# First W1 load split, one warm-up product fewer, third V in another bank, last key sums in two parts and scaled on VectorE

## The chip, the core and the metric

The kernel runs on one core of a Trainium2 chip. The core has five engines with instruction queues of their own: TensorE (PE, matrix products, with a weight loader PEld that overlaps it), VectorE (DVE), ScalarE (ACT), GpSimd (POOL) and SyncE (SP, which here only issues transfers). They meet through semaphores alone. The metric is the device time of one execution in microseconds; a kernel's time is the median of its runs.

## What is computed

The input `x` has 2048 tokens of 512 features. Two branches read it, and a gate per token mixes them.

```python
def reference(A_x, A_wqkv, A_w_phi, A_wo, B_x, B_w1, B_w2, gate_w):   # H = 32 heads of 16
    g = sigmoid((A_x * gate_w).sum(-1, keepdims=True))
    q, k, v = split_heads(A_x @ A_wqkv)
    pq, pk = q @ w_phi, k @ w_phi                                     # per head, 16 x 16
    phi_q = concat([softmax(pq), softmax(-pq)])                       # 32 features per head
    phi_k = concat([softmax(pk), softmax(-pk)])
    kv  = einsum("bhsf,bhsd->bhfd", phi_k, v);  z = phi_k.sum(s)
    o   = (phi_q @ kv) / (phi_q @ z + 1e-6)
    a   = merge_heads(o) @ A_wo
    b   = relu(A_x @ B_w1) @ B_w2                                     # 512 -> 1376 -> 512
    return g * a + (1 - g) * b
```

All tensors are bfloat16; sums are kept in fp32.

## The kernel before

Every engine has a list of operations written in program order (`_Plan`). An operation names the events that it waits for (`after`) and the event that it sets (`ev`); `emit` turns them into semaphore waits. So the order on each engine is the order of the calls in the source, and nothing is rescheduled. A waiting operation holds everything behind it on its engine.

PSUM has 8 banks of 512 fp32 columns. `free[bank]` holds the event after which a bank may be written again, as a rule the copy that emptied it. `nextbank()` hands out banks 3, 4 and 5 in turn. Bank 2 is for the value products `vtile`, banks 0 and 1 are for the q and k products of `atile`, and banks 6 and 7 collect kv over the whole loop.

The stages, in the order of PE's queue:

1. Start. `warm(5)`, `gatecol(3)` and `warm(2)` put products of a constant on PE (L209) while the first loads run; nothing reads them. Then `xtr(0)` and `xtr(1)` transpose the first 512 tokens by products with an identity matrix (L217), eight products for each half of them, and DVE and ACT copy the results into `XT` (L225, L229).
2. First part of the dense branch. `slab(t)`, for t from 0 to 3, multiplies rows t of W1 by the first 512 tokens for eight units u of 128 columns (L490). Each unit accumulates in a bank of its own over the four slabs. Every product of slab t waits for the load `w1{t}`, one transfer of 128 rows and 1376 columns (344 KB). The relus follow, then two more units (`hunit`).
3. Value products and weight preparation. `vtile(0)`, four times `pre` (W_qk times the block-diagonal W_phi, L287), `rest(0)`, four times `pre`, `vtile(1, "dve")`, `vtile(2, "dve")` (products L373, copies on DVE L381).
4. The loop over 16 tiles of 128 tokens. `atile(m)` makes the q and k logits (L307), ACT takes exp of plus and minus the logits (L326), and DVE sums the exponentials of the keys over each softmax group (L339, event `zk`), takes the reciprocal (L342, `rz`), and POOL multiplies (L346, `pk`), which gives the key features. DVE then sums the query exponentials (L351) and takes their reciprocal (L356); POOL scales the positive half against the negative (L358, L360). A DMA transpose on SP's queue brings the query features to `PHQ` (L365). Three tiles later `kv(m)` (L395) accumulates phi_k times v, with a column of ones for z. Units of the dense branch are placed between, by the table `mid`.
5. End of the loop. `kv(13)`, `kv(14)` and `kv(15)` lie between the last units of the dense branch (`late`); `gate()` puts three short DVE operations (L417 to L420) and `kvfin()` four (L404, L408) behind the last tile's sums. In tiles 5, 8, 11, 13, 14 and 15 (`split`) the exponentials are four operations, keys first: `epk`, `emk` (plus and minus keys), then `ep`, `em` (queries). In tile 15 alone the multiplication L346 is in two halves, softmax groups 0 to 31 on POOL and 32 to 63 on DVE.
6. Output. For each tile `nd` (query features times kv and z, L427), the division on DVE (L433, L437), a DMA transpose (L443), `finA` (times W_o, L461), `finB` (times W2, L452), the mix on DVE (L475), and the store.

SP's queue issues, in this order: two loads of x, four of W1 (L154), W_phi, WV, two transposing loads of W_qk, three of x, and then the transposes and stores of the stages above. The load of `gate_w` is on ACT's queue.

The lines around the change:

Of the kernel before, what the change touches and what calls it, by code (L numbers as in the profile page):

```python
# [6 lines left out]
ALU = mybir.AluOpType  # L7
AX = mybir.AxisListType
# [49 lines left out]
def bass_gated_mix__linear_kernel_hedgehog__dense_activation_relu__prompt_kernel(  # L58
# [17 lines left out]
    P = 128  # L76
# [17 lines left out]
    with ExitStack() as es:  # L94
# [55 lines left out]
            p.dma("sp", lambda e: e.dma_start(out=XS[:, 2 * h:2 * h + 2, :], in_=xq[:, 2 * h:2 * h + 2, :]),  # L150
                  f"x0{h}", ev=f"x0{h}")

        def loadw1(t):
            p.dma("sp", lambda e: e.dma_start(  # L154
                out=W1[:, t, 0:DFF], in_=B_w1[t * P:(t + 1) * P, :]), f"w1{t}", ev=f"w1{t}")

        p.dma("act", lambda e: e.dma_start(out=GR[:, :], in_=gate_w.rearrange("(j p) -> j p", p=P)), "gr", ev="gr")
        for h in range(2):
            loadx0(h)
        for t in range(NDT):  # L160
            loadw1(t)
        p.dma("sp", lambda e: e.dma_start(
            out=WPS[:, :, :], in_=A_w_phi.rearrange("(g hl) r c -> (hl r) g c", g=NDT)), "wps", ev="wps")
# [43 lines left out]
        def warm(n, cols=512):  # L207
            for _ in range(n):
                p.op("pe", lambda e: e.matmul(PS[:, 4, 0:cols], ones[:, 0:P], ones[:, 0:cols], start=True, stop=True))  # L209
# [20 lines left out]
                         after=[f"xt{nm}{q}"], ev=f"x{nm}2")  # L230
                    free[bank] = [f"x{nm}2"]

        w1all = [f"w1{t}" for t in range(NDT)]

        def relu(c, kt, bank, eng):
            dst, src = HT[:, kt, c * 512:(c + 1) * 512], PS[:, bank, :]
# [9 lines left out]
        def nextbank():  # L246
            rot[0] += 1
            return 3 + (rot[0] - 1) % 3
# [51 lines left out]
        def atile(m):  # L300
            b = m % NB
            first = xready(m // 4) + ([f"pc{i}" for i in range(8)] if m == 0 else [])
            order = [(dt, w) for dt in range(NDT) for w in range(2)]
            if m - 1 in split:
                order = [(dt, w) for w in (1, 0) for dt in range(NDT)]
            for i, (dt, which) in enumerate(order):
                p.op("pe", lambda e, dt=dt, which=which: e.matmul(  # L307
                    PS[:, which, 0:DE], XT[:, dt, m * P:(m + 1) * P], WQK[:, which, dt * DE:(dt + 1) * DE],
                    start=(dt == 0), stop=(dt == NDT - 1)),
                    after=(first if i == 0 else []) + (free[which] if dt == 0 else []),  # L310
                    ev=(f"qk{m}" if i == 7 else None))
            src = PS[:, 0:2, 0:DE].rearrange("p a (h f) -> p a h f", h=H)
            base = b * 8 * D
            busy = [f"tq{m - NB}", f"pk{m - NB}", f"pq{m - NB}"] if m >= NB else []

            def expo(s, w, ev):
                step = (4 * D, 2 * D)[s]
                off = base + s * (2 * D + 16)
                scale = (1.0, -1.0)[s]
                if w is None:  # L320
                    dst = bass.AP(tensor=EB, offset=off, ap=[[EBS, P], [step, 2], [32, H], [1, FE]])
                    s_ = src
                else:
                    dst = bass.AP(tensor=EB, offset=off + w * step, ap=[[EBS, P], [32, H], [1, FE]])
                    s_ = src[:, w, :, :]
                p.op("act", lambda e: e.activation(dst, s_, ACT.Exp, scale=scale),  # L326
                     after=[f"qk{m}"] + busy, ev=ev)

            if m in split:
                for w, nm in ((1, "k"), (0, "")):  # L330
                    expo(0, w, f"ep{nm}{m}")
                    expo(1, w, f"em{nm}{m}")
            else:
                expo(0, None, f"ep{m}")
                expo(1, None, f"em{m}")
            emk = f"emk{m}" if m in split else f"em{m}"
            free[1] = [emk]
            free[0] = [f"em{m}"]
            p.op("dve", lambda e: e.tensor_reduce(  # L339
                ZB[:, b, 64:128], EB[:, b, 2, :].rearrange("p (g f) -> p g f", f=DH), AX.X, ALU.add),  # L340
                after=[emk, f"cst{b}"], ev=f"zk{m}")
            p.op("dve", lambda e: e.reciprocal(SC[:, b, 64:128], ZB[:, b, 64:128]),  # L342
                 after=[f"zk{m}"] + ([f"pk{m - NB}"] if m >= NB else []), ev=f"rz{m}")
            halves = (("pool", 0, 2 * H),) if m < NT - 1 else (("pool", 0, H), ("dve", H, 2 * H))
            for eng, f0, f1 in halves:
                p.op(eng, lambda e, f0=f0, f1=f1: e.tensor_tensor(  # L346
                    EB[:, b, 3, :].rearrange("p (g f) -> p g f", f=DH)[:, f0:f1, :],
                    EB[:, b, 2, :].rearrange("p (g f) -> p g f", f=DH)[:, f0:f1, :],
                    SC[:, b, 64 + f0:64 + f1].unsqueeze(2).to_broadcast([P, f1 - f0, DH]), ALU.mult),
                    after=[f"rz{m}"] + ([f"kv{m - NB}"] if m >= NB else []), ev=f"pk{m}" + ("b" if f0 else ""))  # L350
            p.op("dve", lambda e: e.tensor_reduce(  # L351
                ZB[:, b, 0:64].rearrange("p (h s) -> p h s", s=2),
                bass.AP(tensor=EB, offset=base, ap=[[EBS, P], [32, H], [2 * D + 16, 2], [1, DH]]), AX.X, ALU.add),
                after=[f"em{m}"] + ([f"sc{m - NB}"] if m >= NB else []), ev=f"zq{m}")
            zq = ZB[:, b, 0:64].rearrange("p (h s) -> p h s", s=2)
            p.op("dve", lambda e: e.reciprocal(SC[:, b, 32:64], zq[:, :, 1]),  # L356
                 after=[f"zq{m}"] + ([f"sc{m - NB}"] if m >= NB else []), ev=f"rq{m}")
            p.op("pool", lambda e: e.tensor_tensor(SC[:, b, 0:32], zq[:, :, 0], SC[:, b, 32:64], ALU.mult),  # L358
                 after=[f"rq{m}"], ev=f"sc{m}")
            p.op("pool", lambda e: e.tensor_tensor(  # L360
                EB[:, b, 0, :].rearrange("p (h s f) -> p h s f", h=H, s=2)[:, :, 1, :],
                EB[:, b, 1, :].rearrange("p (h s f) -> p h s f", h=H, s=2)[:, :, 1, :],
                SC[:, b, 0:32].unsqueeze(2).to_broadcast([P, H, DH]), ALU.mult),
                after=[f"sc{m}"] + ([f"tq{m - NB}"] if m >= NB else []), ev=f"pq{m}")
            p.dma("sp", lambda e: e.dma_start_transpose(  # L365
                out=PHQ[:, :, m * P:(m + 1) * P], in_=EB[:, b, 0, :]),
                f"tq{b}", after=[f"pq{m}", f"cst{b}"] + (["pm7"] if m == 12 else []), ev=f"tq{m}")

        def vtile(m, eng="act"):
            b = m % VB  # L370
            bank = 2
            for dt in range(NDT):
                p.op("pe", lambda e, dt=dt: e.matmul(  # L373
                    PS[:, bank, :], XT[:, dt, m * P:(m + 1) * P], WV[:, dt, :],
                    start=(dt == 0), stop=(dt == NDT - 1)),
                    after=((xready(m // 4) + ["wv"] + free[bank]) if dt == 0 else ()),
                    ev=(f"v{m}" if dt == NDT - 1 else None))
            dst, src = VS[:, b, :, 0:64], PS[:, bank, :].rearrange("p (g c) -> p g c", g=NG)
            after = [f"v{m}"] + ([f"kv{m - VB}"] if m >= VB else [])
            if eng == "dve":  # L380
                p.op("dve", lambda e: e.tensor_copy(dst, src), after=after, ev=f"cv{m}")  # L381
            else:
                p.op("act", lambda e: e.activation(dst, src, ACT.Copy), after=after, ev=f"cv{m}")  # L383
            free[bank] = [f"cv{m}"]

        def kv(m):
            b = m % NB
            vb = m % VB
            for g in range(NG):
                after = []  # L390
                if g == 0:
                    after = [f"pk{m}", f"cv{m}", f"one{vb}"] + ([f"pk{m}b"] if m == NT - 1 else [])
                    if m == 0:
                        after += free[6] + free[7]
                p.op("pe", lambda e, g=g: e.matmul(  # L395
                    PS[:, 6 + g // 4, (g % 4) * GW:(g % 4) * GW + 65],
                    EB[:, b, 3, g * P:(g + 1) * P], VS[:, vb, g, 0:65],
                    start=(m == 0 and g % 4 == 0), stop=(m == NT - 1), skip_group_check=True),
                    after=after, ev=(f"kv{m}" if g == NG - 1 else None))
# [88 lines left out]
        def slab(t):  # L488
            for u in range(8):
                p.op("pe", lambda e, u=u: e.matmul(  # L490
                    PS[:, UB[u], :], W1[:, t, u * P:(u + 1) * P], XT[:, t, 0:512],
                    start=(t == 0), stop=(t == NDT - 1)),
                    after=[f"w1{t}", XA[t], XB[t]] + free[UB[u]],
                    ev=(f"h0_{u}" if t == NDT - 1 else None))

        warm(5)
        gatecol(3)
        warm(2)
        xtr(0)
        xtr(1)  # L500
        for b in range(VB):
# [17 lines left out]
        for i in range(4, 8):  # L519
            pre(i)  # L520
        vtile(1, "dve")
        vtile(2, "dve")
        mid = [[(1, 0), (1, 1)], [(1, 2), (1, 3)], [(1, 4), (1, 5)], [(1, 6), (1, 7)], [(1, 8), (1, 9)], [(2, 0)],
               [(1, -1), (2, 1)], [(2, 2), (2, 3)], [(2, 4)], [(2, -1), (2, 5)], [(2, 6), (2, 7)], [(2, 8)],
               [(3, -1), (2, 9)], [(3, 0), (3, 1)], [(3, 2), (3, 3)], []]
# [113 lines left out]
```

## Time and profile before

| | us |
|---|---|
| median of 13 runs | 151.45 |
| lowest and highest | 150.79, 153.94 |
| profiled execution, its own time | 151.68 |
| its span, first to last instruction | 149.9 |
| PE busy in the span | 144.4 |
| DVE, ACT, POOL busy | 92.6, 72.1, 53.6 |

The profile is of one execution. A group of instructions is named by its line, its engine, and what it reads and writes. A matmul's shown length goes on for the time that its result takes through the array, so consecutive ones overlap; the step from start to start is the time that one takes from PE. A wait is put down to the work that ended last before the waiting instruction could go on. The chain that ended last runs back from the final instruction through whatever released each step. "Idle" of an engine that does not set the end costs nothing.

### The profile page before, as it was taken

How to read it: one execution, taken by the hardware profiler on the slowest of the kernel's cores; microseconds unless marked ns; L12 is line 12 of the kernel's file. 1: busy time of each engine (PE TensorE's matmuls, PEld its weight loads, DVE VectorE, ACT ScalarE, POOL GpSimd, SP SyncE). 2: the span in 40 equal slices, each digit the busy share in tenths (PEclk: the TensorE clock that was granted, in tenths of full speed). 3: DMA queues.
4: the chain of work that ended last, by engine and by line, in shares of the span. 5: the costliest groups of instructions: out<-in, count | busy, mean ns of one | idle time of the engine just before them, and what ended most of it. 6: DMA issues, size and time to landing. Idle time of an engine off the chain costs nothing.

```text
span 149.9 us, 2544 instructions
## 1 busy us (share of the span) xinstructions
PE 144.4 (96%) x979; PEld 73.4 (49%) x979; DVE 92.6 (62%) x156; ACT 72.1 (48%) x123; POOL 53.6 (36%) x63
## 2 busy tenths in 40 slices
PE   7799979999999999999999989999999999999992
PEld 2544734444455554645645544545544444444442
DVE  2526852778878678678698895475444555555242
ACT  3306527777778797877878863011222111111150
POOL 2030000777768678877879872000000000000000
PEclk9999999999999999999999999999999999999999
DMA  4999994033328977334743436533333322322312
GB/s 140 326 255 225 208 155 90 0 70 70 74 62 238 232 201 107 70 70 105 42 105 70 105 70 39 105 70 105 74 87 85 74 70 70 74 70 72 83 62 70
DMA packets 44516, 16.11 MB, mean 108 GB/s; under 512 B 39288, under 2 KB 43736, under 8 KB 44504
## 3 DMA queue, kind: packets, MB, share of 16 engines
q1 hardware_dynamic: 44352, 15.92, 49.4%
q8 instruction: 8, 0.13, 0.4%
q10 hardware_dynamic: 152, 0.03, 0.1%
q14 instruction: 4, 0.03, 0.1%
HBM read 4.41 MB, written 2.10 MB: 43 GB/s over the span
## 4 chain that ended last, share of the span: by engine, by line
PE 90%; DMA 3%; DVE 2%; POOL 1%; ACT 1%; SPq 1%; issue 0%
PE PS L452 25%; PE PS L307 17%; PE PS L253 16%; PE PS L373 9%; PE PS L461 9%; PE PS L490 5%; DMA W<-in_B_w_dram 3%; PE PS L427 3%; PE PS L395 2%; PE PS L265 2%; PE PS L287 1%; POOL EB L346 1%; DVE ZB L339 1%; ACT EB L326 1%; DVE WQK L475 1%; SPq L150 1%
## 5 line engine op out<-in xcount | busy, mean ns | idle before, releaser
L452 PE MATMUL PS<-W,HT 128*128 128x512 bf16 (+4 forms) x187 | 40.6, 366 | 0.0
L346 POOL TENSOR_TENSOR EB<-EB,SC 128x1024 bf16<-128x1024 bf16 (+1 forms) x16 | 30.5, 1905 | 26.8 <-DVE SC L342 26.8
L326 ACT ACTIVATE EB<-PS 128x480 bf16<-128x480 f32 (+1 forms) x44 | 30.1, 757 | 16.9 <-PE PS L307 16.9
L466 ACT ACTIVATE TFA<-PS,GT 128x512 bf16<-128x512 f32 x16 | 11.0, 687 | 42.7 <-PE PS L461 36.6
L253 PE MATMUL PS<-XT,W 128*128 128x512 bf16 x128 | 30.7, 379 | 0.0
L307 PE MATMUL PS<-WQK,XT 128*128 128x480 bf16 x128 | 28.5, 366 | 0.0
L339 DVE TENSOR_REDUCE ZB<-EB 128x64 f32<-128x1024 bf16 x16 | 19.5, 1220 | 14.2 <-ACT EB L326 14.2
L475 DVE SCALAR_TENSOR_TENSOR WQK<-PS,OMG,TFA 128x512 bf16<-128x512 f32 (+2 forms) x17 | 12.2, 719 | 23.6 <-ACT TFA L466 22.4
L452 PEld LDWEIGHTS PS<-W,HT 128*128 128x128 bf16 (+1 forms) x187 | 17.0, 98 | 17.4
L239 ACT ACTIVATE HT<-PS 128x512 bf16<-128x512 f32 x35 | 20.3, 617 | 8.3 <-PE PS L490 5.8
L307 PEld LDWEIGHTS PS<-WQK,XT 128*128 128x128 bf16 x128 | 12.5, 98 | 13.8
L351 DVE TENSOR_REDUCE ZB<-EB 128x64 f32<-128x1024 bf16 x16 | 18.6, 1164 | 0.0
L253 PEld LDWEIGHTS PS<-XT,W 128*128 128x128 bf16 x128 | 12.0, 98 | 13.2
L360 POOL TENSOR_TENSOR EB<-EB,SC 128x512 bf16<-128x512 bf16 x16 | 16.9, 1055 | 1.3
L373 PE MATMUL PS<-WV,XT 128*128 128x512 bf16 x64 | 16.4, 379 | 0.8 <-DVE VS L381 0.8
L461 PE MATMUL PS<-WO,OT 128*128 128x512 bf16 x64 | 16.1, 378 | 0.0
L437 DVE TENSOR_TENSOR WQK<-PS,RDEN 128x512 bf16<-128x512 f32 x16 | 11.1, 691 | 0.5
L461 PEld LDWEIGHTS PS<-WO,OT 128*128 128x128 bf16 x64 | 6.1, 97 | 7.2
L342 DVE RECIPROCAL SC<-ZB 128x64 f32<-128x64 f32 x16 | 8.8, 553 | 0.5
L433 DVE RECIPROCAL RDEN<-PS 128x32 f32<-128x32 f32 x16 | 5.6, 350 | 4.7 <-PE PS L427 4.7
L373 PEld LDWEIGHTS PS<-WV,XT 128*128 128x128 bf16 x64 | 5.4, 97 | 5.9 <-DVE VS L381 1.3
L383 ACT ACTIVATE VS<-PS 128x512 bf16<-128x512 f32 x13 | 8.0, 612 | 0.0
(54 smaller groups left out, 88.1 us busy)
## 6 DMA issues: line engine op xcount, KB each, us to landing
out_dram<-WQK SPq DMA_DIRECT2D x15, 128.0 KB, 1.7
W<-in_B_w_dram SPq DMA_DIRECT2D x4, 344.0 KB, 5.7
W<-in_B_w_dram SPq DMA_DIRECT2D x1, 768.0 KB, 4.9
OT<-in_A_x_dram SPq DMA_DIRECT2D x2, 256.0 KB, 3.0
WV<-in_A_wqkv_dram SPq DMA_DIRECT2D x1, 512.0 KB, 7.1
W<-in_B_w_dram SPq DMA_DIRECT2D x1, 512.0 KB, 5.6
WO<-in_A_wo_dram SPq DMA_DIRECT2D x1, 512.0 KB, 3.9
PHQ<-EB SPq DMA_TRANSPOSE x16, 2.8
```

The source lines that it names most:

```text
L239: p.op("act", lambda e: e.activation(dst, src, ACT.Relu), after=[f"h{c}_{kt}"], ev=ev)
L253: p.op("pe", lambda e, t=t: e.matmul(PS[:, bank, :], W1[:, t, kt * P:(kt + 1) * P], XT[:, t, c * 512:(c + 1) * 512], start=(t == 0), stop= ...
L307: p.op("pe", lambda e, dt=dt, which=which: e.matmul(PS[:, which, 0:DE], XT[:, dt, m * P:(m + 1) * P], WQK[:, which, dt * DE:(dt + 1) * DE] ...
L326: p.op("act", lambda e: e.activation(dst, s_, ACT.Exp, scale=scale), after=[f"qk{m}"] + busy, ev=ev)
L339: p.op("dve", lambda e: e.tensor_reduce(ZB[:, b, 64:128], EB[:, b, 2, :].rearrange("p (g f) -> p g f", f=DH), AX.X, ALU.add), after=[emk, ...
L346: p.op(eng, lambda e, f0=f0, f1=f1: e.tensor_tensor(EB[:, b, 3, :].rearrange("p (g f) -> p g f", f=DH)[:, f0:f1, :], EB[:, b, 2, :].rearra ...
L351: p.op("dve", lambda e: e.tensor_reduce(ZB[:, b, 0:64].rearrange("p (h s) -> p h s", s=2), bass.AP(tensor=EB, offset=base, ap=[[EBS, P], [ ...
L360: p.op("pool", lambda e: e.tensor_tensor(EB[:, b, 0, :].rearrange("p (h s f) -> p h s f", h=H, s=2)[:, :, 1, :], EB[:, b, 1, :].rearrange( ...
L373: p.op("pe", lambda e, dt=dt: e.matmul(PS[:, bank, :], XT[:, dt, m * P:(m + 1) * P], WV[:, dt, :], start=(dt == 0), stop=(dt == NDT - 1)), ...
L452: p.op("pe", lambda e, kt=kt, M=M: e.matmul(PS[:, bank, 0:n], HT[0:M, kt, m * P:(m + 1) * P], W2[0:M, kt, cs], start=(kt == 0), stop=(kt = ...
L461: p.op("pe", lambda e, t=t: e.matmul(PS[:, bank, :], OT[:, t, m * P:(m + 1) * P], WO[:, t, :], start=(t == 0), stop=(t == NDT - 1)), after ...
L475: p.op("dve", lambda e: e.scalar_tensor_tensor(out=OSB[:, ob, cs], in0=PS[:, bank, 0:n], scalar=OMG[:, m:m + 1], in1=TFA[:, m % 2, cs], op ...
```

## The change

There are five edits.

- The first W1 slab is loaded in two transfers: columns 0 to 511 (units 0 to 3, event `w10a`, 128 KB) and then columns 512 to 1375 (event `w10`, 216 KB). Products of slab 0 with u below 4 wait for the first alone.
- `warm(2)` becomes `warm(1)`.
- `vtile(2, "dve")` writes the bank that `nextbank()` gives, which is 3 at that place, instead of bank 2. Each later call of `nextbank()` thereby gives the next bank of the three.
- In tile 15 the sum over key groups becomes two operations of half the size: over the plus exponentials after `epk15`, and over the minus exponentials after `emk15`.
- In tile 15 the multiplication of the keys is one operation on DVE over all 64 groups, instead of one half on POOL and one half on DVE; `kv(15)` no longer waits for a second event.

```diff
-        def loadw1(t):
+        def loadw1(t, c0=0, c1=DFF, tag=""):
             p.dma("sp", lambda e: e.dma_start(
-                out=W1[:, t, 0:DFF], in_=B_w1[t * P:(t + 1) * P, :]), f"w1{t}", ev=f"w1{t}")
+                out=W1[:, t, c0:c1], in_=B_w1[t * P:(t + 1) * P, c0:c1]), f"w1{t}{tag}", ev=f"w1{t}{tag}")
...
-        for t in range(NDT):
+        loadw1(0, 0, 4 * P, "a")
+        loadw1(0, 4 * P)
+        for t in range(1, NDT):
             loadw1(t)
...
-        w1all = [f"w1{t}" for t in range(NDT)]
+        w1all = ["w10a"] + [f"w1{t}" for t in range(NDT)]
...
-            p.op("dve", lambda e: e.tensor_reduce(
-                ZB[:, b, 64:128], EB[:, b, 2, :].rearrange("p (g f) -> p g f", f=DH), AX.X, ALU.add),
-                after=[emk, f"cst{b}"], ev=f"zk{m}")
+            zk = ZB[:, b, 64:128].rearrange("p (h s) -> p h s", s=2)
+            ek = EB[:, b, 2, :].rearrange("p (h s f) -> p h s f", h=H, s=2)
+            if m == NT - 1:
+                for s, nm in ((0, "epk"), (1, "emk")):
+                    p.op("dve", lambda e, s=s: e.tensor_reduce(zk[:, :, s], ek[:, :, s, :], AX.X, ALU.add),
+                         after=[f"{nm}{m}", f"cst{b}"], ev=f"zk{m}" if s else None)
+            else:
+                p.op("dve", lambda e: e.tensor_reduce(zk, ek, AX.X, ALU.add),
+                     after=[emk, f"cst{b}"], ev=f"zk{m}")
...
-            halves = (("pool", 0, 2 * H),) if m < NT - 1 else (("pool", 0, H), ("dve", H, 2 * H))
-            for eng, f0, f1 in halves:
-                p.op(eng, lambda e, f0=f0, f1=f1: e.tensor_tensor(
-                    EB[:, b, 3, :].rearrange("p (g f) -> p g f", f=DH)[:, f0:f1, :],
-                    EB[:, b, 2, :].rearrange("p (g f) -> p g f", f=DH)[:, f0:f1, :],
-                    SC[:, b, 64 + f0:64 + f1].unsqueeze(2).to_broadcast([P, f1 - f0, DH]), ALU.mult),
-                    after=[f"rz{m}"] + ([f"kv{m - NB}"] if m >= NB else []), ev=f"pk{m}" + ("b" if f0 else ""))
+            p.op("pool" if m < NT - 1 else "dve", lambda e: e.tensor_tensor(
+                EB[:, b, 3, :].rearrange("p (g f) -> p g f", f=DH),
+                EB[:, b, 2, :].rearrange("p (g f) -> p g f", f=DH),
+                SC[:, b, 64:128].unsqueeze(2).to_broadcast([P, 2 * H, DH]), ALU.mult),
+                after=[f"rz{m}"] + ([f"kv{m - NB}"] if m >= NB else []), ev=f"pk{m}")
...
-        def vtile(m, eng="act"):
+        def vtile(m, eng="act", bank=2):
             b = m % VB
-            bank = 2
...
-                    after = [f"pk{m}", f"cv{m}", f"one{vb}"] + ([f"pk{m}b"] if m == NT - 1 else [])
+                    after = [f"pk{m}", f"cv{m}", f"one{vb}"]
...
-                    after=[f"w1{t}", XA[t], XB[t]] + free[UB[u]],
+                    after=["w10a" if t == 0 and u < 4 else f"w1{t}", XA[t], XB[t]] + free[UB[u]],
...
-        warm(2)
+        warm(1)
...
-        vtile(2, "dve")
+        vtile(2, "dve", nextbank())
```

## The prediction

> **What bounds the kernel now.** I read the page first: TensorE (PE) is busy 144.4 of 149.9 us, and no other engine passes 62%.
>
> ```profile
> PE 144.4 (96%) x979; PEld 73.4 (49%) x979; DVE 92.6 (62%) x156; ACT 72.1 (48%) x123; POOL 53.6 (36%) x63
> ```
>
> So an edit pays only where PE stands still, and costs only where it makes PE stand still. The list of waits, kept to PE and its weight loader, says where that is.
>
> ```profile
> PEld PS L490 <- DMA W<-in_B_w_dram: 1.1, 1, 1.1
> PEld PS L395 <- POOL EB L346: 0.9, 1, 0.9
> PE PS L490 <- DMA W<-in_B_w_dram: 0.9, 1, 0.9
> PE PS L373 <- DVE VS L381: 0.8, 1, 0.8
> PE PS L395 <- POOL EB L346: 0.4, 1, 0.4
> ```
>
> Three places: the first W1 product waits for its load, the third V product for a copy, the last kv product for the scaled keys. The chain that ended last, in order of time (start, length, what), passes through all three.
>
> ```profile
> 1.66 5.01 DMA W<-in_B_w_dram
> 6.72 7.08 PE PS L490 x32
> ...
> 18.90 0.88 PE PS L373 x4
> 19.80 0.70 DVE VS L381
> 20.55 1.04 PE PS L373 x4
> ...
> 84.54 1.04 ACT EB L326 x2
> 85.60 1.23 DVE ZB L339
> 86.86 0.56 DVE SC L342
> 87.49 1.57 POOL EB L346
> 89.11 0.42 PE PS L395 x8
> 89.53 1.73 PE PS L253 x8
> 91.26 0.25 PE PS L427 x8
> ```
>
> From 21.4 to 88.5 us the windows view gives PE 67.1 us busy of 67.1: in the loop the other engines follow PE, so time saved ahead of it reaches the end whole. Matmul lengths include a pipeline tail; the step between starts is what counts: 8 products of 512 columns in 1.73 us are 0.216 us each. The timeline shows the slow start: seven warm-up products start 0.427 us apart, and 16 transposes of 128 columns from 3.94 to 5.54 us, 0.107 us apart, both half speed; the 32 W1 products from 6.72 us step at 0.216. The clock row prints 1.0 throughout because the clock record begins only at 6.52 us.
>
> **Third V in another bank.** vtile(2) wrote bank 2 and waited for vtile(1)'s copy. vtile(1)'s products begin at 18.73 us in the timeline, so PE is free at 18.73 + 4 x 0.216 = 19.59, and vtile(2) starts at 20.55: 0.96 us idle. Its new bank is 3, last emptied by a relu (ACT, 14.70 + 0.60 = 15.30 us), long before. The next customer, atile(0), would start at 19.59 + 0.86 = 20.45 and needs the copies of pre (DVE 17.04 + 2.42 = 19.46, ACT 18.45 + 1.06 = 19.51): ready. vtile(2)'s copy is queued on DVE behind vtile(1)'s and ends near 21.2, ahead of its first user. All later turns of banks 3, 4, 5 move by one and keep their period; finB(0) on bank 4 then waits for a relu two units earlier than before. Gain 0.96, with no cover to lose.
>
> **One warm-up fewer.** It gives 0.43 us of PE time, but the second half of x lands only at 1.19 + 3.5 = 4.69 us (slower of the two loads at L150). The first eight transposes move from 3.94 to 3.54, the second eight only from 4.79 to 4.72. The cast that slab 0 needs (third at L225, ending 5.89) ends near 5.82. By itself this is worth nothing: PE waits for W1 until 6.67. It matters for what follows.
>
> **Slab 0 in two loads.** SP issues one more DMA, 0.43 us (four at L154 in 1.85), so W_phi, WV, the wqk transposes, the x transposes and the later transposes on that queue all go 0.43 later. Cover: the second wqk transpose lands near 9.2 + 6.6 = 15.8, then 16.2, and pre(4), at 17.83, comes at 17.3: 1.1 us of slack. WV (11.1) and Wbd (11.6) have over 3 us. The first x transpose lands at 13.43 + 5.8 = 19.2, then 19.7, and is wanted at 24.07 less 1.5. None shows.
>
> When does the 128 KB part land? The whole 344 KB landed 6.67 - 4.69 = 1.98 us after x, but the four W1 loads then follow 0.98 us apart (1.66 + 5.0 to 3.1 + 6.5, three steps). So 1.0 us of the 1.98 was start cost. The part needs 0.98 x 128/344 = 0.37 us of transfer: 5.06 us if the start cost falls on the second part, 6.06 if on the first, 6.67 if time goes by rows rather than bytes (both parts have 128). I take 5.9, by the nearest row (the whole load, start cost mostly first). Here the Trainium skill speaks against the change: "DMA: Bandwidth & Descriptors", section "Bandwidth", advises batching and gives 0.95 us for 64 KB and 6.15 for 1 MB (issued from GpSimd), about 0.6 us of it fixed. By that rule part one lands near 6.0 and the rest 0.6 late, at 7.3; by the row above, where a load queued behind another shows no such gap, near 6.8. I take the row.
>
> Slab 0 then starts at 5.9 instead of 6.72. The four products that part one feeds run at half speed until the clock opens at 6.52: 0.62 / 0.427 = 1.45 of them, and 2.55 x 0.216 = 0.55 more, done at 7.07. The fifth product stood at 6.72 + 4 x 0.216 = 7.58: gain 0.51. The rest (6.8) is there; slab 1's load (about 7.7) is wanted at 7.93. The skill's "TensorE: Matmul & The Clock Gate", Part 1, says that the array starts at half rate and opens after about 3.4 us of sustained work, in a window that runs free of the kernel. So 6.52 is this execution's moment: where it comes before 5.9, the four end at 6.76 and the load at 6.8 decides, gain 0.78; where it comes later, see the last rival. Taken: 0.55, near the profiled execution.
>
> **Last key sums and scaling.** Now the DVE timeline of that stage (start, length).
>
> ```profile
> 84.93 0.35 DVE L356 RECIPROCAL SC<-ZB 128x32 f32<-128x32 f32 x1
> 85.60 1.22 DVE L339 TENSOR_REDUCE ZB<-EB 128x64 f32<-128x1024 bf16 x1 [0.32 <-ACT EB L326]
> 86.86 0.55 DVE L342 RECIPROCAL SC<-ZB 128x64 f32<-128x64 f32 x1
> 87.45 0.69 DVE L346 TENSOR_TENSOR EB<-EB,SC 128x512 bf16<-128x512 bf16 x1
> 88.06 1.21 DVE L351 TENSOR_REDUCE ZB<-EB 128x64 f32<-128x1024 bf16 x1
> 90.84 0.17 DVE L408 SCALAR_TENSOR_TENSOR KVNZ<-PS,M 128x16 bf16<-128x16 f32 x1
> ```
>
> Two things stand there: kv(15) waits for POOL's half (87.49 + 1.56 = 89.05), and behind it DVE has no pause until kvfin ends at 91.01, just as PE reaches nd(0) at 91.09. Before: PE is free for kv(15) at 86.81 + 8 x 0.216 = 88.54, starts at 89.11: 0.57 idle. After: the first sum needs epk15 (about 85.06) but DVE is busy until 85.28, so it starts at 85.30. A half sum costs between 0.61 (half the row) and 0.69 (the 512-element row); I take 0.66, two end at 86.64 (was 86.82). Reciprocal 86.68 to 87.23. The whole scaling costs between 1.22 (the 1024-element sum) and 1.39 (twice 0.69); taken 1.23, since both rows hold a fixed part: 87.27 to 88.50. kv(15) then starts at 88.54 without a stall, and PE reaches nd(0) 0.57 us sooner, at 90.52.
>
> But the next thing is late. Queued behind the scaling on DVE are the query sum, its reciprocal, the three gate operations and kvfin. The query sum starts at 88.42 instead of 88.06, and so kvfin's parts end 0.36 later: the first pair at 90.95, the second at 91.37. nd(0) waits for the one before its first product and for the other before its fifth; its last four (0.13 us) end at 91.54, against 91.35 before. The stall is moved, not removed: net loss 0.19; with the low costs 0.08, with the high ones 0.41. POOL's part of the old split freed DVE, and that is lost.
>
> **Sum.** -0.96 - 0.55 + 0.19 = -1.32 us. The profiled execution took 151.68 (span 149.9 and 1.8 around it), so 150.36; the median of the runs is 151.45, 0.23 under it: 150.1.
>
> **Rivals.** (a) The load goes by rows: part one lands at 6.67, the rest up to 0.98 later, near 7.65 against a need at 7.58. The front gains nothing: -0.96 + 0.19 + 0.07, 150.7. For it: the slow first load. Against: loads of equal rows and unequal bytes are not in this trace. (b) The V bank doesn't do what it says: the wait reappears at atile(0). The ready times above speak against it; then -0.36 is left, less rotation trouble: near 151.3. (c) Slower: the clock opens one window late. The clock record is 143.36 us long from 6.52, which is 42 x 3.413. In the window from 3.10 to 6.52 PE streamed 2 x 0.427 + 16 x 0.107 = 2.56 us, 75%, and the clock opened; in the one before 5 x 0.427, 63%, and it did not. After the change it is 0.43 + 1.71 + (6.52 - start): 81% for a start at 5.9, 75% at 6.1, 63% at 6.5. So it decides if part one lands after 6.1 to 6.5. Then PE is at half speed until 9.93: from 6.3 it does 8.5 products where before had done 14.9; 6.4 x 0.216 = 1.38 lost, -0.96 + 1.38 + 0.19 = +0.61, 152.1. Without the removed warm-up the share would be higher.
>
> **How the numbers follow.** Main case 0.69 (its own range 149.6 to 150.6: front 0.78 or 0.3, end 0.08 or 0.41); (a) 0.17; (b) 0.04; (c) 0.10. About 0.2% (0.3 us) is what a measurement of this kernel can tell from no change. Faster: main and (a), 0.86; same: (b), 0.04; slower: (c), 0.10. The range 149.5 to 151.0 holds main and (a) with the high end cost, and leaves out (b) and (c).
>
> **What would show it.** Third V: L373 starts 0.86 us after the second, no wait on DVE. Front: W1's first product near 5.9 with steps of 0.43, then 0.216, the fifth near 7.1; wrong if it starts at 6.6 or the half-speed steps go on. End: kv(15) with no wait, and a new wait of PE on DVE's kvfin at nd(0), 0.8 us in two pieces; wrong if nd(0) follows its units directly. The prediction fails if the loads after the split land later than PE wants them, or if steps of 0.43 last beyond 7 us.

## The result, and the profile after

The changed kernel takes 150.38 us (median of 11 runs, 150.09 to 151.06), the kernel before 151.51 in the 48 runs beside it. The ratio is 0.9938, with an interval of 0.9921 to 0.9955: 0.94 us faster, between 0.68 and 1.20. The forecast was 1.32 us faster. The direction holds and the time lies in the range; 0.38 us of the gain is missing. Some executions of most of these kernels take over 1.5% longer than the fastest; the medians count them, and the ratios and the differences worked out from the ratios do not.

The profiled execution took 149.81 us, with a span of 148.0 and 1.8 around it as before. The first line of the page of the changed kernel, busy time of each engine:

```profile
PE 143.3 (97%) x978; PEld 72.9 (49%) x978; DVE 93.0 (63%) x157; ACT 72.0 (49%) x123; POOL 52.0 (35%) x62
```

The list of waits of the changed kernel, PE and its weight loader (us in total, times, longest):

```profile
PEld PS L495 <- DMA W<-in_B_w_dram: 0.7, 1, 0.7
...
PEld PS L432 <- issue: 0.7, 1, 0.7
...
PE PS L495 <- DVE XT L227: 0.5, 1, 0.5
...
PE PS L432 <- DVE KVNZ L413: 0.2, 1, 0.2
```

The waits of L373 on DVE and of L395 on POOL are gone. A wait at the first W1 product is left, and there is a new one at nd (L432, which was L427) on `kvfin`. The chain that ended last of the changed kernel, in order of time (start, length, what), passes through none of the three old stops:

```profile
5.16 0.14 issue
5.30 7.07 PE PS L495 x32
...
17.46 1.73 PE PS L378 x8
19.19 1.01 PE PS L309 x5
```

Slab 0 starts at 5.30 instead of 6.72, and what released it is not its load but the cast of x on DVE. The eight V products of tiles 1 and 2 (L378) follow each other in 1.73 us, where before a copy of DVE stood between them. From there on the changed kernel is 2.4 us ahead in these two executions (1.42 from the front and 0.96 from V). At the last DVE operation it still is: that ends at 145.20 instead of 147.62. The last operations of DVE, before and then after:

```profile
146.65 0.97 DVE L475 SCALAR_TENSOR_TENSOR WQK<-PS,OMG,TFA 128x384 bf16<-128x384 f32 x2 [1.13 <-PE PS L452]
```

```profile
144.23 0.97 DVE L480 SCALAR_TENSOR_TENSOR WQK<-PS,OMG,TFA 128x384 bf16<-128x384 f32 x2 [1.13 <-PE PS L457]
```

But the span then lasts 2.81 us more, where it lasted 2.26 before. What lies in these last microseconds is the store of the last tile's last 128 columns, on ACT's queue. The transfers view of the kernel before (queue: packets, MB, share; issue: count, size, median us to landing), and SP's waits (for whom: us in total, times, longest):

```profile
q14 instruction: 4, 0.03, 0.1%
...
out_dram<-WQK ACTq DMA_DIRECT2D x1, 32.0 KB, 1.5
```

```profile
SPq L51 <- DMA out_dram<-WQK: 1.3, 1, 1.3
```

The same two views of the changed kernel:

```profile
q14 instruction: 5, 0.04, 0.1%
...
out_dram<-WQK ACTq DMA_DIRECT2D x1, 32.0 KB, 2.3
```

```profile
SPq L51 <- DMA out_dram<-WQK: 2.3, 2, 1.3
```

The last store lands 2.3 us after its issue instead of 1.5, SP's end waits a second time for it, and the queue that fetches instructions has one packet more in the span. The forecast has no term for any of this. The experiments had to say whether it belongs to the change.

### The profile page after: what moved, and what is told of

It is laid out like the page before. It is cut to its first block, busy times and chain, and to the rows that moved or that the text cites. A ratio compares the mean times of both kernels' runs of the same rounds, so it can differ in the third digit from the quotient of the medians.

```text
span 148.0 us, 2543 instructions
## 1 busy us (share of the span) xinstructions
PE 143.3 (97%) x978; PEld 72.9 (49%) x978; DVE 93.0 (63%) x157; ACT 72.0 (49%) x123; POOL 52.0 (35%) x62
## 4 chain that ended last, share of the span: by engine, by line
PE 89%; DVE 6%; issue 2%; ACT 1%
PE PS L457 25%; PE PS L309 16%; PE PS L255 14%; PE PS L466 9%; PE PS L378 9%; PE PS L495 5%; PE PS L432 3%; PE PS L211 2%; PE PS L267 2%; PE PS L400 2%; DVE ZB L357 2%; PE PS L289 1%; DVE ZB L348 1%; DVE XT L227 1%; ACT EB L328 1%
## 5 line engine op out<-in xcount | busy, mean ns | idle before, releaser
L352 POOL TENSOR_TENSOR EB<-EB,SC 128x1024 bf16<-128x1024 bf16 x15 | 28.9, 1928 | 24.2 <-DVE SC L350 24.2
L348 DVE TENSOR_REDUCE ZB<-EB 128x64 f32<-128x1024 bf16 x15 | 18.3, 1220 | 13.9 <-ACT EB L328 13.9
L357 DVE TENSOR_REDUCE ZB<-EB 128x64 f32<-128x1024 bf16 x16 | 18.6, 1164 | 0.0
L378 PE MATMUL PS<-WV,XT 128*128 128x512 bf16 x64 | 16.2, 378 | 0.0
L432 PEld LDWEIGHTS PS<-KVNZ,PHQ 128*128 128x128 bf16 x128 | 6.0, 97 | 4.1 <-issue 0.7
```

The source lines that it names most:

```text
L348: p.op("dve", lambda e: e.tensor_reduce(zk, ek, AX.X, ALU.add), after=[emk, f"cst{b}"], ev=f"zk{m}")
L352: p.op("pool" if m < NT - 1 else "dve", lambda e: e.tensor_tensor(EB[:, b, 3, :].rearrange("p (g f) -> p g f", f=DH), EB[:, b, 2, :].rearr ...
L357: p.op("dve", lambda e: e.tensor_reduce(ZB[:, b, 0:64].rearrange("p (h s) -> p h s", s=2), bass.AP(tensor=EB, offset=base, ap=[[EBS, P], [ ...
L378: p.op("pe", lambda e, dt=dt: e.matmul(PS[:, bank, :], XT[:, dt, m * P:(m + 1) * P], WV[:, dt, :], start=(dt == 0), stop=(dt == NDT - 1)), ...
```

## The experiments

The theory was the forecast's sum: V bank -0.96, front -0.55, end stage +0.19. Each part was first run alone, on the kernel before.

**V bank alone.**

```diff
-        vtile(2, "dve")
+        vtile(2, "dve", nextbank())
```

> The kernel before with the third V in the next bank, nothing else. Theory (idle time of TensorE is worth its length): 0.96 us less, ratio 0.9937, and the third V's products follow the second's with no wait. Rival (the wait only moves to the first attention tile, or the later bank turns cost): less than 0.3 us, ratio above 0.998.

Measured: 150.67 us (22 runs) against 151.42, ratio 0.9933 (0.9917 to 0.9949): -1.01 us. The timeline of this kernel (start, length, operation, count) has the eight V products in one group and the first q and k products right behind them, 1.73 us after the first:

```profile
18.62 1.89 PE L372 MATMUL PS<-WV,XT 128*128 128x512 bf16 x8
20.35 1.78 PE L307 MATMUL PS<-WQK,XT 128*128 128x480 bf16 x8
```

So this one edit is worth as much as the whole change (-0.94), and the other four together should give about nothing.

**Key sums and scaling alone.**

```diff
+            if m == NT - 1:
+                for s, nm in ((0, "epk"), (1, "emk")):
+                    p.op("dve", lambda e, s=s: e.tensor_reduce(zk[:, :, s], ek[:, :, s, :], AX.X, ALU.add),
...
-            halves = (("pool", 0, 2 * H),) if m < NT - 1 else (("pool", 0, H), ("dve", H, 2 * H))
...
+            p.op("pool" if m < NT - 1 else "dve", lambda e: e.tensor_tensor(
```

> The kernel before with the last key sums in two parts and their whole scaling on VectorE, nothing else. Theory as predicted: kv(15) starts without its wait of 0.57 us, but VectorE's queue ends later and TensorE waits at the first output product instead, net +0.19 us (0.08 to 0.41). After the profile of the changed kernel, where this stage came out even: -0.02 us. Rival (the removed wait is a gain): -0.5 us.

Measured: 151.38, ratio 0.9994 (0.9975 to 1.0012): -0.09 us, from -0.38 to +0.18. The forecast's +0.19 is just outside, its low case of +0.08 is inside; the runs can't tell this edit from no change. The timeline of this kernel shows where the stall went:

```profile
87.60 0.41 PE L399 MATMUL PS<-VS,EB 128*128 128x65 bf16 x8
87.85 1.89 PE L253 MATMUL PS<-XT,W 128*128 128x512 bf16 x8
89.94 0.63 PE L431 MATMUL PS<-KVNZ,PHQ 128*128 128x68 bf16 x8 [0.20 <-DVE KVNZ L412]
90.40 2.32 PE L456 MATMUL PS<-W,HT 128*128 128x512 bf16 x10
```

The last kv products (L399) and the units (L253) run without a pause, and nd (L431) stands before its first and its fifth product. From the first kv product of the stage at 83.41 to finB (L456) at 90.40 it takes 6.99 us; the kernel before takes 7.02 between the same two:

```profile
84.33 0.66 PE L395 MATMUL PS<-VS,EB 128*128 128x65 bf16 x16
...
91.35 1.02 PE L452 MATMUL PS<-W,HT 128*128 128x512 bf16 x4
```

**Warm-up alone, split alone, and both.**

```diff
-        warm(2)
+        warm(1)
```

> The kernel before with one warm-up product fewer, nothing else. Theory: nothing within 0.1 us, since TensorE waits for the whole first W1 load anyway. Rival (the missing product makes the clock open later): slower by up to 1 us, with steps of 0.43 us among the first W1 products in some executions.

Measured: 151.43, ratio 1.0007 (0.9981 to 1.0034). Nothing, as forecast.

```diff
-        for t in range(NDT):
+        loadw1(0, 0, 4 * P, "a")
+        loadw1(0, 4 * P)
+        for t in range(1, NDT):
```

> The kernel before with the first W1 slab in two loads, both warm-ups kept. Theory: like the front edits together, about -0.5 us of TensorE idle at the start given back by +0.5 us in the final store, so 0 within 0.2 us; first W1 product some 0.07 us later than without the warm-up. Rival (the removed warm-up made the front gain nothing by keeping the clock low): -0.5 us.

Measured: 151.61, ratio 1.0011 (0.9998 to 1.0023). No gain, and the two edits together:

> The kernel before with the first W1 slab in two loads and one warm-up fewer, nothing else. Theory: -0.55 us, between -0.3 and -0.8 by the moment at which the clock opens; in the profile the first W1 product starts before 6.1 us and the first load lands a good part of a microsecond ahead of the second. Rival (the gain of the profiled changed kernel, 1.4 us, is the rule and not a lucky execution): -1.4 us. Rival (loads go by rows): 0.

Measured: 151.47, ratio 1.0007 (0.9983 to 1.0031): +0.1 us where -0.55 was expected. The front's whole gain is missing here. Yet the traces of both front kernels showed slab 0 starting earlier, and both, like the changed kernel, have a last store of 2.3 us and a fifth instruction packet; those of V bank, end stage and warm-up have 1.5 us and four. What the front has and the others lack is one more transfer on SP's queue.

**One more transfer on SP, elsewhere.** The kernel before, with the ten row blocks of W2 that are loaded in tile 3 cut into three transfers instead of two. The front is untouched, and no other engine's list changes, since `finB` waits for one count that all loads of W2 raise.

```diff
-                for i in range(2):
-                    a, b = (0, 6) if i == 0 else (6, KU)
+                for i in range(3):
+                    a, b = ((0, 6), (6, 8), (8, KU))[i]
```

> The kernel before with one more transfer on SyncE's queue far from the start: the second W2 load in two. Nothing at the front is touched. Theory (one more SyncE instruction moves an 8 KB instruction fetch into the last store, whose last piece then lands late): +0.5 us, the end of the span 2.75 us after the last VectorE operation instead of 2.25, and the fetch near the last store. Rival (the late last store belongs to the split of W1, or is chance): 0 us and 2.25 us.

Measured: 151.93 against 151.5, ratio 1.0044 (1.0027 to 1.0061): +0.67 us. Its transfers view:

```profile
q14 instruction: 5, 0.04, 0.1%
...
out_dram<-WQK ACTq DMA_DIRECT2D x1, 32.0 KB, 2.4
```

The cut is in the middle of the loop, the load of W2 is wanted much later, and still the last store, 100 us on, lands late. So the cost goes with one more transfer on SP, not with the split of W1.

**The changed kernel with one transfer less.** The ten row blocks of W2 come in one transfer, so that SP issues as many as before.

```diff
-                for i in range(2):
-                    a, b = (0, 6) if i == 0 else (6, KU)
+                for i in range(1):
+                    a, b = (0, KU)
```

> The changed kernel with the two W2 loads of ten row blocks in one, so that SyncE's queue has as many instructions as before the change. Theory: the fetch is again after the last store and 0.5 us come back, ratio to the kernel before about 0.990. Rival: as the changed kernel, 0.9938.

Measured: 150.07, ratio 0.9908 (0.9885 to 0.9932): -1.39 us (-1.74 to -1.03). The store is back at 1.5 us and the packets at four.

**The front with one transfer less**, the same edit of W2 on the kernel with split and `warm(1)` alone:

> The kernel before with the split first W1 load and one warm-up fewer, and with one W2 load of ten row blocks for two, so that SyncE's queue keeps its length. Theory (the front edits are worth about 0.5 us and the last store takes them back): -0.5 us, ratio 0.9967, end of the span 2.25 us after the last VectorE operation. Rival (the front edits themselves are worth nothing, since TensorE only waits for the next slab's load instead): 0 us.

Measured: 150.93 against 151.59, ratio 0.9962 (0.995 to 0.9975): -0.58 us (-0.76 to -0.38), where the front with SP's extra transfer gave +0.1. The instruction queue has four packets again, and the last store in the transfers view is:

```profile
out_dram<-WQK ACTq DMA_DIRECT2D x1, 32.0 KB, 1.5
```

**The control**: the kernel before with the ten row blocks of W2 in one transfer, to see whether that edit is a gain of its own.

> Control: the kernel before with one W2 load for two, nothing else; SyncE has one instruction fewer than before. Theory: 0 us within 0.15, because the fetch was after the last store already. Rival (fewer transfers are a gain by themselves): -0.3 us or more.

Measured: 151.78, ratio 1.0016 (0.9998 to 1.0035): +0.24 us (-0.03 to +0.53), no gain, and perhaps a small loss, which would make the front's own worth larger than 0.58. Without the extra transfer there is nothing to win back. In the kernel before, the last fetch of instructions is recorded at 150.03 us, behind the last store.

**The query part of the last tile late.** The runs point at two repairs: no extra transfer, and the new wait at nd. That wait is on DVE, where the query sum and reciprocal of tile 15 stand ahead of `kvfin`; nothing needs them until the output of tile 15. Here they, POOL's scaling and the transpose behind it are emitted after `nd(1)`, on top of the changed kernel with one transfer less.

```diff
+            def query():
...
+            if m < NT - 1:
+                query()
+            else:
+                late_query.append(query)
```

> As the run with one W2 load, and in tile 15 the query sum, its reciprocal, the POOL scaling and the transpose are placed behind nd(1), so that kvfin stands right behind the key scaling on VectorE. Theory: TensorE finds kvfin done at the first output product, and the stall of about 0.55 us goes, ratio about 0.986. Rival (the moved operations hold the divisions of the output tiles and SyncE's transposes, and TensorE waits there): no better than the run with one W2 load.

Measured: 149.47 (6 runs), ratio 0.9888 (0.9845 to 0.9931). The timeline of this kernel in the same stage:

```profile
82.26 0.66 PE L408 MATMUL PS<-VS,EB 128*128 128x65 bf16 x16
...
86.70 1.89 PE L255 MATMUL PS<-XT,W 128*128 128x512 bf16 x8
88.43 0.42 PE L440 MATMUL PS<-KVNZ,PHQ 128*128 128x68 bf16 x8
88.68 2.54 PE L465 MATMUL PS<-W,HT 128*128 128x512 bf16 x10
```

On DVE `kvfin` ends at 87.83. nd (L440) starts at 86.70 + 8 x 0.216 = 88.43, straight behind the units, and the stage takes 88.68 - 82.26 = 6.42 us against 6.99 of the end stage run alone: 0.57 less, the size of the stall that the change only moved. The interval is wide; the same kernel again:

> The changed kernel with one W2 load and the query part of tile 15 placed behind nd(1), the same as the run before it, for a narrower interval. Theory: ratio 0.987, 1.0 us under the changed kernel (0.5 from the last store, 0.55 from the stall at the first output product). Rival: 0.991, only the last store came back.

Measured: 149.43 (6 runs) against 151.59, ratio 0.9873 (0.9843 to 0.9904): 1.92 us faster than the kernel before and about 1 us faster than the changed one. This version beats both. Against the run with one transfer less (0.9908) its intervals overlap, so the 0.57 of the late query part rests on the traces; the two runs put it at 0.30 and 0.53.

**The changed kernel again**, beside these:

> The changed kernel once more, beside the others on the same chip. Theory: ratio 0.994 as on record; another profile of the start, in which TensorE waits either for the first slab or for the second slab's load, and the end of the span 2.75 us after the last VectorE operation.

Measured: 150.33 (7 runs), ratio 0.9938 (0.9915 to 0.9961), the first result repeated. In its profiled execution (150.81 us) the clock record begins at 6.68, and the timeline shows the front nearly as the forecast drew it:

```profile
3.51 2.13 PE L219 MATMUL PS<-IDN,OT 128*128 128x128 bf16 x16
5.83 2.73 PE L495 MATMUL PS<-XT,W 128*128 128x512 bf16 x10 [0.18 <-DVE XT L227]
```

Slab 0 starts at 5.83 with steps of 0.38 and 0.42 us before the record begins, 0.25 and 0.21 after, and the fifth product starts at 7.09.

The parts add up. V bank -1.01, front -0.58, end -0.09, SP's extra transfer +0.67: -1.01, against -0.94 (-0.68 to -1.20) measured. Without the extra transfer they come to -1.68, and the run showed -1.39 (-1.74 to -1.03), so that its nearness to the forecast's -1.32 is in part chance. The extra transfer is worth 0.67 us alone, 0.68 with the front and 0.45 in the changed kernel. The two sums without the scaling, the scaling without the two sums, the split with both warm-ups and one transfer less, and the late query part with W2 in two loads were not run.

## Why the prediction was right, and where it failed

**Third V in another bank: right.** Forecast -0.96, measured -1.01, by the mechanism given: products without a gap, and no new customer waits. Rival (b) is out.

**One warm-up fewer: right.** Nothing by itself, and the pair with and without it (1.0007 and 1.0011) can't be told apart.

**Slab 0 in two loads, its gain: right in size, not in its working.** -0.55 forecast, -0.58 once SP's transfer is taken out (the split with one warm-up fewer). But the landing of part one was costed at 5.9 and that of the rest at 6.8. In the eight traces with the split, part one landed at 4.6 to 5.3 us, and the rest at 5.3 to 5.8. The whole load had landed at 5.5 to 6.7 in the six without it. So the two parts together landed earlier than the one load did in most traces. The row used was 0.6 us or more too late for the first part and 1.0 for the rest. The rule of the Trainium skill against splitting (page "DMA: Bandwidth & Descriptors", section "Bandwidth") is to batch transfers; the estimate worked out from its table, 6.0 and 7.3, was later still. Rival (a), loads by rows, is out. Slab 0 then starts 0.14 to 0.15 us after the cast of x in every split trace: the load has stopped being the limit. Now the transposes of x set its start, and these come sooner without the warm-up: the cast ends at 5.15 to 5.75 us in the seven split traces without it, at 5.89 in the one with it. That the 5.9 came out well in the repeated run (5.83) is due to the cast, which the forecast placed at 5.82 and did not use.

Part of the gain is given back at slab 1. Its load landed between 6.3 and 8.5 us, and in four of the eight split traces PE stood there. The chain of the kernel with the split alone shows it:

```profile
2.60 5.87 DMA W<-in_B_w_dram
8.47 0.05 issue
8.52 3.84 PE PS L492 x17
```

Slab 1 starts at 8.52 with PE waiting, where the forecast wanted its load at 7.93 and had it at 7.7. This is what the forecast had named as its way to fail, and it happens in some executions. In these traces the last product of the slabs ends between 12.4 and 13.9 us (mean 13.1 with the split, 13.4 without), so single traces can't carry the 0.58; the timed runs do.

**The clock: as read, and rival (c) was not put to the test.** The profile's clock record began at 6.52 before and at 3.76 after. Over the other traces it begins anywhere from 3.6 to 6.7 us, with and without the split. That agrees with the Trainium skill's "TensorE: Matmul & The Clock Gate", Part 1, that the window runs free of the kernel. The forecast's working of the windows holds in all 13 records, with matmuls taken at 0.427 us for 512 columns: in the 3.41 us ahead of each opening PE streamed for 75% or more, in the 3.41 us before those for 67% or less. (The records are 143.36 or 146.77 us long, which differ by 3.41.) Rival (c) asked for a start of slab 0 after 6.1; the eight split traces have it between 5.30 and 6.03, and in none did half-speed steps last beyond 7.1. The 1.42 us at the front of the profiled pair, against 0.58 by the runs, was luck: in that execution of the changed kernel the clock record begins early, so that the fifth product starts at 6.16 (7.09 in the repeated run), the second half of x landed at 4.11 us (4.67 before), and slab 1's load at 6.30, in time.

**Slab 0 in two loads, its cost: the step that failed.** The forecast went through every queue entry behind the extra transfer, found the slack of each, and wrote "None shows". For the transfers that holds: none of those landings is waited for. But with one more transfer on SP a fetch of 8 KB of instructions fell into the span's last microseconds, and the last store, which ends the kernel, lands 0.8 us later. This costs 0.67 us measured alone. Five traces have the extra transfer (the changed kernel twice, split, split with one warm-up fewer, W2 in three): all show 2.3 to 2.4 us and five packets. The nine others show 1.5 us and four; in them the fetch comes 0.1 us or more after the end of the span. Added to the forecast's -1.32, it gives -0.65; the runs say -0.94, and the rest of the difference is the next point. So the total came out inside its range partly because two misses, +0.67 here and -0.28 there, offset each other.

How the fetch delays the store can be read from the packets in the traces. In the changed kernel 15 of the 16 pieces of the last store arrive between 146.58 and 146.83 us and one at 147.52. The store is 128 packets of 256 bytes. The fetch packet runs from 146.30 to 146.79, and the last eight packets of the store follow from 146.78, after a gap of 0.4 us. The other four traces with the extra transfer show the same: the fetch packet takes from 0.39 to 0.56 us, and each time the last eight packets start within 0.01 us of its end. So one sixteenth of the store stood behind the fetch. The trace does not name the transfer engine of a packet, but five matches at five different lengths leave little room for another cause. What stays open is whose instructions the packet held, and why one more transfer brings it forward by that much.

**Last key sums and scaling: the stall moved as forecast, the size was off.** As forecast, kv(15) follows without a wait, and PE stops at nd(0) in two pieces. The chain of the changed kernel there:

```profile
88.24 0.09 DVE KVNZ L413
88.33 0.14 issue
88.47 0.29 PE PS L432 x4
88.75 0.04 issue
88.80 0.30 PE PS L432 x4
89.10 2.38 PE PS L457 x11
```

The term +0.19 rested on `kvfin` coming 0.36 us later, behind two half sums and the whole scaling. The timeline of DVE in the changed kernel:

```profile
82.53 0.35 DVE L362 RECIPROCAL SC<-ZB 128x32 f32<-128x32 f32 x1
82.80 1.22 DVE L345 TENSOR_REDUCE ZB<-EB 128x32 f32<-128x512 bf16 x2
84.06 0.55 DVE L350 RECIPROCAL SC<-ZB 128x64 f32<-128x64 f32 x1
84.64 1.23 DVE L352 TENSOR_TENSOR EB<-EB,SC 128x1024 bf16<-128x1024 bf16 x1
85.79 1.21 DVE L357 TENSOR_REDUCE ZB<-EB 128x64 f32<-128x1024 bf16 x1
88.57 0.17 DVE L413 SCALAR_TENSOR_TENSOR KVNZ<-PS,M 128x16 bf16<-128x16 f32 x1
```

The scaling is 1.23 to the digit. The two half sums take 1.22 us together, no more than the one whole sum of 1.22 before. They also begin at 82.80, while the reciprocal ahead of them (82.53 + 0.35) still runs; the forecast let them begin behind it. So the query sum starts 85.79 - 82.14 = 3.65 us after ACT's exponentials of the stage begin, against 88.06 - 84.54 = 3.52 before: 0.13 late, not 0.36. The stage from there to finB takes 6.79 us against 6.81. The term is -0.02 by the traces and -0.09 (-0.38 to +0.18) by the runs, where +0.19 was forecast.

## What to carry to other kernels

Count the instructions that an edit adds to each queue, even to one with slack everywhere: here one transfer more on SP cost 0.67 us at the other end of the kernel, and merging two loads that nobody waited for brought it back. Compare how long the last store takes in both profiles before explaining a front or a loop. When a wait is taken from one place, read what stands in that engine's queue ahead of the next thing PE needs, and move what is not needed yet: here an edit worth nothing became, by the traces, worth 0.57 us.

## What was not expected of the hardware

- Instructions are fetched by transfers that share the span with the kernel's own. The Trainium skill says in "Runtime: NRT & Kernel Launch", section "Instruction fetch mechanics", that the sequencer streams them and that the cost is mostly hidden. For the four packets earlier in the span no wait shows, which agrees; the fifth held up a sixteenth of the last store and goes with 0.67 us.
- A load of 344 KB in two parts of 128 and 216 KB landed whole at 5.3 to 5.8 us in eight traces, in one part at 5.5 to 6.7 in six. Why was not settled.
- Two sums of half the size took 1.22 us on DVE, as long as the one of full size (1.22), since the second begins 0.08 us before the first ends (0.63 and 0.68 us each).
- The moment at which the clock record begins moved by 3 us from execution to execution (3.64 to 6.68), and with it whether the first slab starts at full or half speed (steps of 0.22 or about 0.4 us).
